# RWKV-7 recurrence and hard-swish layer: the decay scans of units 4 and 5 at another place in the order

## The chip, the cores and the metric

The kernel runs on one core of a Trainium2 chip. The metric is device microseconds of one execution. The engines are TensorE (PE; PEld is its weight load), VectorE (DVE), ScalarE (ACT), GpSimd (POOL) and SyncE (SP), which here only issues DMAs. Each engine works through its own instructions in the order of the program and waits where an operand or a buffer isn't ready.

## The reference

The input is r, k, v, w, a, b, each of 4 batches, 8 heads, 768 steps and 40 elements. For each batch and head a 40 x 40 state is carried through the steps:

```
for t in range(S):
    y[:, :, t] = einsum('bhd,bhde->bhe', rt, state)
    Sa = einsum('bhde,bhe->bhd', state, at)
    state = state * wt - outer(Sa, bt) + outer(vt, kt)
```

The result, reshaped to 3072 rows of 320, is x of a dense layer: h = x @ w_in (320 x 2048), g = h * clip(h + 3, 0, 6) / 6, out = g @ w_out (2048 x 320). The output is float32. The two weight matrices come in as 64-bit floats, which the kernel converts itself.

## The kernel before, in words

**Units.** The 768 steps are cut into blocks of 64. A unit is a pair of batches and one block: names[i] gives its block and pair. Four units make a group (NU = 4), two blocks by two pairs, and there are 24. Inside a unit the recurrence is written as matrix products. Scaling by the cumulated decay makes this possible; it is what the change moves.

**prepare(i)** (L534) makes what a unit needs apart from the state. Its stages that matter here:
- "W" (w_stage, L537): four TensorE transposes of the unit's w into a PSUM tile (L484), two copies into wm, one of them reversed (L545/L549 on VectorE or L547/L551 on ScalarE, by the unit's number), the load of a later unit's w (`fetch("W", following(i))`, L553: two DMAs on SyncE), and a scan into prods on VectorE (L555).
- "gam" (gam_stage, L560): a reciprocal (L564) and a scan backward (L566) on VectorE, then gam and rgam, the cumulated decay and its inverse: one half of each copied from wm by VectorE (L579, for units from 4 on), the other half from prods by GpSimd (L583, L584), and dec, by GpSimd too (L586).
- "A" (L593): transposes of a, which VectorE multiplies by gam into at (L599). "B" (L602) does the same for b and rgam (L607). "K", "F", "factor", "E" and "EV" follow.

**step(i)** (L832) carries the state through a unit: RT, VT (transposes), C, R, S, U, UT, rS (r against the old state), sn (the state sum, L961 and L969), H, y (L984; VectorE adds ys in L995 and GpSimd multiplies by gam in L996 into yg), and move, move2: eight DMAs on SyncE, four each (L1010, L1015), that bring yg into the layout of the dense layer (xt).

**Dense layer and weights.** feed_forward() (L1039) cuts the dense layer into pieces: h matmuls (L1066), ScalarE and VectorE for the hard-swish (L1081, L1082), o matmuls (L1107). pieces(n) issues n of them. load_weights() (L312) converts the weights in 20 parts: loads on SyncE (L334), three ScalarE activations each (power(), L384 to L386), three VectorE instructions each (L369, L372, L360). A piece may be issued only when its weights are converted in program order.

**Order.** The kernel fixes the order of every engine by hand. Around the change it is PLAN (L1282), a text of 16 lines. A word such as "2UT:1" runs stage UT of unit 2's step, with one part of the weight conversion dealt at its matmuls; X and Y are blocks of the first inversion; P and Q stand for prepare(4) and prepare(5) and run first "W", then "gam". From the ninth line on (t = 8) the PSUM for the dense layer is taken, and pieces and the second group's other stages (by_twos, L1197) go between the lines. By then ps_any (L119) hands out only two kinds of PSUM bank in turn: "one", which exists once, and a "pair", which exists twice.

```
1303  chains.update({x: in_turn(prepare(NU + n, None), ["W", "gam"]) for n, x in enumerate("PQ")})
1317          if t == BEGIN:
1318              fetch("A", NU + 1)
1319              fetch("W", NU + 3)
...
1331          if t >= BEGIN:
1332              next(second_group)
```

**Buffers the steps touch.** w of units 4 and 6 use one buffer (inputs["W"]); w of unit 5 is loaded early into values[4], the buffer that v of unit 4 gets later. ys and yg share two buffers (tag "yg"): unit 3's yg (L947, L990) gets the one that unit 2's yg leaves once its moves are done. wm exists twice, gam six times, rgam and prods twice.

Of the kernel before, what the change touches and what calls it, by code (L numbers as in the profile page):

```python
# [17 lines left out]
P = 128  # L18
# [13 lines left out]
def kernel(  # L32
# [47 lines left out]
    NU = 2 * NP  # L80
# [361 lines left out]
    def fetch(name, i, engine=None):  # L442

        if i is None or i >= NK:
            return
        x, crossed = {"W": (w, 0), "A": (a, 0), "B": (b, 0), "K": (k, 0), "R": (r, 1),
                      "V": (v, 1)}[name]
        if name == "V":
            t = values[i % AHEAD]
        else:  # L450
            t = placed.get((name, i))
            if (name, i) == ("R", 1):
                t = others["K"]
            if (name, i) == ("W", NU + 1):
                t = values[NU]
            t = t if t is not None else (others if i < 2 * NU and i % 2 and name != "R" else inputs)[name]
        g, p = names[i]
        engines = engine or nc.sync
        for q in range(2):
            engine = engines[q] if isinstance(engines, tuple) else engines  # L460
            y = x[2 * p + q, :, g * BL:(g + 1) * BL, :]
            rows = slice(q * BL, (q + 1) * BL)
            if crossed:
                for s in range(2):
                    engine.dma_start(out=t[rows, 4 * s:4 * s + 4, 0:D],
                                     in_=y[s::2].rearrange("h t e -> t h e"))
            else:
                engine.dma_start(out=t[rows, :, 0:D], in_=y.rearrange("h t e -> t h e"))  # L468
        data[i][name + "N"] = t

    def following(i):

        if i < 2:
            return None
        if i < 2 * NU:

            return i + 2 if i % NU < NU - 2 or i % 2 == 0 else None
        return i + 1

    def turn_pairs(x):  # L480

        o = ps_any([P, NPR, P])
        for n in range(NPR):
            nc.tensor.transpose(out=o[:, n, :],  # L484
                                in_=x[:, 2 * n:2 * n + 2, :].rearrange("p s e -> p (s e)"),
                                identity=ident[:])
        return o
# [46 lines left out]
    def prepare(i, F):  # L534
        n, o = i % NU, data[i]
        halves = i >= 2 * NU
        def w_stage():  # L537
            wt = turn_pairs(o["WN"])
            yield PE

            wm = o["wm"] = wms[i % 2]
            wv = wm[:, 0:SCAN].rearrange("p (r m i) -> p r m i", m=2, i=HB + 1)
            x = wt[:].rearrange("p r (q m i) -> p (r q) m i", q=2, m=2)
            if i in (0, NU, NU + 1):
                nc.vector.tensor_copy(wv[:, :, 0, 1:HB + 1], x[:, :, 0, ::-1])  # L545
            else:
                nc.scalar.activation(out=wv[:, :, 0, 1:HB + 1], in_=x[:, :, 0, ::-1], func=AF.Copy)  # L547
            if i in (0, NU, NU + 1):
                nc.vector.tensor_copy(wv[:, :, 1, 1:HB + 1], x[:, :, 1, :])  # L549
            else:  # L550
                nc.scalar.activation(out=wv[:, :, 1, 1:HB + 1], in_=x[:, :, 1, :], func=AF.Copy)  # L551
            if i != NU + 1:
                fetch("W", following(i))  # L553
            prods = o["prods"] = tmp.tile([P, NB, 2, HB + 1], F32, name="prods", bufs=2)
            nc.vector.tensor_tensor_scan(  # L555
                out=prods[:].rearrange("p r m i -> p (r m i)"), data0=wm[:, 0:SCAN], data1=start[:],
                initial=0.0, op0=ALU.mult, op1=ALU.add,
            )
# [135 lines left out]
        def ev_stage():  # L694
# [10 lines left out]
            for x in range(2):  # L705
                nc.scalar.activation(out=EV[half(x)], in_=ev[2][half(x)][:, ::-1] if x else ev[2][half(x)],  # L706
                                     func=AF.Copy)
            o["EV"] = EV

        return {"W": w_stage, "gam": gam_stage, "A": a_stage, "B": b_stage, "F": f_by_32 if i < 2 * NU else f_by_64,  # L710
                "factor": factor_stage, "K": k_stage, "E": e_stage, "EV": ev_stage}

# [559 lines left out]
    def block(i, j):  # L1272

        if i % NU < 2:
            if j == 0:
# [4 lines left out]


    PLAN = """X X:2 0U:4 0UT:2 1R  # L1282
              0sn:2 0H:1 Y:2 P
              1U 1UT:2 0y P
              2RT:1 Y:1 Q
              1sn:1 1H:1 2VT:2 0move 0move2
              1y:2 2R Q
              2S:3 3RT:2
              1move 1move2 2U:3 2UT:1 2C:5
              3R:4 3VT  # L1290
              2rS:3 2sn:3 2H:4 3S:2
              2y:3 3U:1 3UT:10 3C:5
              3rS:1 3sn:2 3H:4 2move
              3y:1 2move2

              3move
              3move2"""
# [191 lines left out]
```

## Time and profile before

| | |
|---|---|
| median of three runs | 792.41 us (791.11 to 794.02) |
| profiled execution | 788.99 us, its span 787.3 us |
| TensorE | 723.7 us busy, 92% of the span, 15832 matmuls |
| VectorE | 496.1 us, 63% |
| ScalarE | 320.0 us, 41% |
| GpSimd | 175.0 us, 22% |
| mean granted TensorE clock | 0.972 of full speed |
| chain that ended last, by engine | PE 77%, DVE 8%, issue 5%, SPq 4%, DMA 3%, ACT 2%, POOL 1% |

The page cuts the span in 40 equal slices and gives each engine's busy share in tenths, 9 for 90% or more. The timeline lists instructions in order of time: start and length in us, engine, line, operation, output and inputs by tile name, how many were merged, and in brackets the idle time of the engine before it and what ended that. A row of busy times by stretch gives for each stretch the busy us and count of each engine, the granted clock, the DMA share and GB/s. SPq is SyncE's issuing of DMAs. W loads appear as W<-in_w_dram for inputs["W"] and as WA<-in_w_dram for a second buffer that units 5 and 7 use.

### The profile page before, as it was taken

The numbers are of one execution on the slowest core, as the hardware profiler recorded it, in microseconds if no ns is written. First come the engines' busy times: TensorE is split into PE (matmuls) and PEld (weight loads), VectorE is DVE, ScalarE is ACT, GpSimd is POOL, SyncE is SP. The second block draws the span as 40 slices with busy tenths as digits, with TensorE's granted clock in tenths as the row PEclk, the third lists the DMA queues.
The fourth block names the chain that finished last, engine by engine and source line by source line (L and its number), as shares of the span: only waits on it lengthen the run. The fifth ranks groups of instructions, "written<-read, shape, count | busy, mean of one in ns | idle before, by whom it ended". The sixth has DMA issues, their size and how long they took to land.

```text
span 787.3 us, 35307 instructions
## 1 busy us (share of the span) xinstructions
PE 723.7 (92%) x15832; PEld 614.3 (78%) x15832; DVE 496.1 (63%) x971; ACT 320.0 (41%) x664; POOL 175.0 (22%) x318
## 2 busy tenths in 40 slices
PE   4626679999999989999999999999999999999998
PEld 3625668778778878888888888888888888888886
DVE  7899995598545699345888445987435982323210
ACT  2377982214445324444334534335534224412211
POOL 6403113122222304112404212304312201000000
PEclk9856999999999999999999999999999999999999
DMA  9684554411332313223213223213221101110000
GB/s 123 115 194 129 127 153 69 75 26 29 55 68 54 66 25 58 51 43 66 46 30 64 45 48 62 50 28 64 45 55 34 33 8 30 30 30 10 14 19 17
DMA packets 174215, 45.03 MB, mean 57 GB/s; under 512 B 157424, under 2 KB 172784, under 8 KB 174064
## 3 DMA queue, kind: packets, MB, share of 16 engines
q1 hardware_dynamic: 169760, 42.03, 27.8%
q8 instruction: 125, 2.05, 1.1%
q10 hardware_dynamic: 4304, 0.74, 0.7%
q14 instruction: 26, 0.21, 0.1%
HBM read 34.08 MB, written 3.93 MB: 48 GB/s over the span
## 4 chain that ended last, share of the span: by engine, by line
PE 77%; DVE 8%; issue 5%; SPq 4%; DMA 3%; ACT 2%; POOL 1%; DVEq 0%; POOLq 0%; ACTq 0%
PE h L1066 27%; PE o L1107 24%; PE pair L522 4%; PE pair L984 3%; PE pair L494 2%; PE pair L961 2%; PE one L484 2%; SPq L468 2%; PE pair L906 2%; PE pair L868 2%; DVE prod L753 1%; DVE x L759 1%; PE pair L926 1%; PE pair L942 1%; PE pair L701 1%
## 5 line engine op out<-in xcount | busy, mean ns | idle before, releaser
L1066 PE MATMUL h<-xt,win 128*128 128x128 f32 (+1 forms) x2304 | 249.2, 282 | 2.8 <-DVE gt L1082 2.0
L1066 PEld LDWEIGHTS h<-xt,win 128*128 128x128 f32 (+1 forms) x2304 | 229.9, 191 | 19.8 <-issue 5.0
L1107 PE MATMUL o<-wout,gt 128*128 128x320 f32 x768 | 230.4, 443 | 0.0
L1107 PEld LDWEIGHTS o<-wout,gt 128*128 128x128 f32 x768 | 138.4, 190 | 50.3 <-issue 0.2
L1082 DVE SCALAR_TENSOR_TENSOR gt<-gt,h 128x512 f32<-128x512 f32 x96 | 62.0, 681 | 71.4 <-ACT gt L1081 71.3
L1081 ACT ACTIVATE gt<-h,three 128x512 f32<-128x512 f32 x96 | 62.1, 685 | 101.9 <-PE h L1066 101.4
L996 POOL TENSOR_TENSOR yg<-ys,gam 128x512 f32<-128x512 f32 x22 | 39.0, 1774 | 156.3 <-DVE ys L995 83.6
L753 DVE TENSOR_TENSOR prod<-x 128x30 f32<-128x30 f32 (+9 forms) x180 | 67.2, 373 | 8.8 <-POOL x L738 3.3
L674 POOL TENSOR_TENSOR KBt<-K,rgt 128x320 f32<-128x320 f32 x22 | 19.0, 866 | 215.6 <-ACT rgt L663 177.8
L759 DVE TENSOR_TENSOR x<-x,prod 128x30 f32<-128x30 f32 (+9 forms) x180 | 62.2, 346 | 5.5
L969 DVE TENSOR_TENSOR state<-pair,state 40x320 f32<-40x320 f32 (+1 forms) x43 | 20.9, 487 | 60.8 <-PE pair L961 34.5
L530 DVE COPY_PREDICATED score<-mask,pair 128x512 f32<-128x512 int32 x72 | 50.6, 723 | 0.5
L995 DVE TENSOR_TENSOR ys<-pair,ys 128x512 f32<-128x512 f32 x22 | 15.2, 691 | 42.9 <-PE pair L701 21.8
L566 DVE TENSOR_TENSOR_SCAN wm<-wm,start 128x528 f32<-128x528 f32 x24 | 37.5, 1562 | 0.8
L555 DVE TENSOR_TENSOR_SCAN prods<-wm,start 128x528 f32<-128x528 f32 x24 | 30.1, 1259 | 10.4 <-ACT wm L551 10.3
L846 ACT ACTIVATE RT<-pair 128x512 f32<-128x512 f32 x22 | 13.1, 596 | 52.8 <-PE pair L494 52.8
L706 ACT ACTIVATE EV<-pair 64x320 f32<-64x320 f32 x44 | 19.0, 431 | 33.7 <-PE pair L701 23.0
L821 ACT ACTIVATE tinv<-pair 32x256 f32<-32x256 f32 x48 | 17.9, 374 | 31.7 <-PE pair L811 31.1
L1125 ACT ACTIVATE ob<-o 128x320 f32<-128x320 f32 x22 | 9.6, 435 | 49.4 <-PE o L1107 29.6
L583 POOL COPY gam<-prods 128x256 f32<-128x256 f32 x24 | 22.0, 916 | 30.7 <-DVE prods L555 26.9
L872 DVE TENSOR_TENSOR RR<-pair,EV 128x320 f32<-128x320 f32 x22 | 10.7, 487 | 25.4 <-PE pair L522 25.4
L984 PE MATMUL pair<-score,KBt 64*64 64x64 f32 x1408 | 25.9, 221 | 0.5 <-issue 0.5
(272 smaller groups left out, 1066.1 us busy)
## 6 DMA issues: line engine op xcount, KB each, us to landing
V<-in_v_dram SPq DMA_DIRECT2D x96, 40.0 KB
out_dram<-ob SPq DMA_DIRECT2D x47, 80.0 KB
R<-in_r_dram SPq DMA_DIRECT2D x92, 40.0 KB
B<-in_b_dram SPq DMA_DIRECT2D x42, 80.0 KB
K<-in_k_dram SPq DMA_DIRECT2D x42, 80.0 KB
W<-in_w_dram SPq DMA_DIRECT2D x37, 80.0 KB
A<-in_a_dram SPq DMA_DIRECT2D x37, 80.0 KB
xt<-yg SPq DMA_DIRECT2D x72, 40.0 KB
```

The costliest lines, as they stand in the source:

```text
L522: nc.tensor.matmul(out=o[i][half(q), n, :], lhsT=lhs[half(i, D), n ^ (2 * q * swap), half(q)], rhs=rhs[half(i, D), n, half(q)], start=True ...
L530: nc.vector.copy_predicated(out=x[:].rearrange("p (i h) t -> p i h t", i=2), mask=mask8, data=o[2])
L555: nc.vector.tensor_tensor_scan(out=prods[:].rearrange("p r m i -> p (r m i)"), data0=wm[:, 0:SCAN], data1=start[:], initial=0.0, op0=ALU.m ...
L566: nc.vector.tensor_tensor_scan(out=back, data0=back, data1=start[:], initial=0.0, op0=ALU.mult, op1=ALU.add)
L753: nc.vector.tensor_tensor(out=pv, in0=_ap(x[:], (i + 1) * L + i, [[L, n], [0, i]]), in1=_ap(x[:], i * L, [[0, n], [1, i]]), op=ALU.mult,)
L759: nc.vector.tensor_tensor(out=rest, in0=rest, in1=pv, op=ALU.add)
L984: nc.tensor.matmul(out=y[q][half(s), pr, :], lhsT=o[name][half(q), h * D:h * D + SLOT], rhs=m[name][half(q), 4 * rs + 2 * s + j, :], start ...
L996: nc.gpsimd.tensor_tensor(out=yg[:], in0=m["ys"][:].rearrange("p r q t -> p r (q t)"), in1=o["G"][:], op=ALU.mult)
L1066: nc.tensor.matmul(out=hp[c][:, i, :], lhsT=lhsT, rhs=rhs, start=(begun[c] == 0), stop=(begun[c] == 3 * NQ - 1))
L1081: nc.scalar.activation(out=gt[:], in_=hp[c][:], func=AF.Relu, bias=three[:], scale=1.0)
L1082: nc.vector.scalar_tensor_tensor(out=gt[:], in0=gt[:], scalar=6.0, in1=hp[c][:], op0=ALU.min, op1=ALU.mult)
L1107: nc.tensor.matmul(out=op[:], lhsT=gts[c][:, n, :], rhs=wout[:, c * HJ + r * NQ + n, :], start=((split or r == 0) and c == 0 and n == 0), ...
```

## The change

P and Q, the "W" and "gam" stages of units 4 and 5, leave the lines of PLAN in which units 0 and 1 step, and stand in the two lines that end unit 3: "W" of both behind 3H and ahead of 2move, "gam" of both behind 3y and ahead of 2move2. With them the two copies of "W" for these units go from VectorE to ScalarE, as for all other units but unit 0.

```diff
-            if i in (0, NU, NU + 1):
+            if i == 0:
                 nc.vector.tensor_copy(wv[:, :, 0, 1:HB + 1], x[:, :, 0, ::-1])
             else:
                 nc.scalar.activation(out=wv[:, :, 0, 1:HB + 1], in_=x[:, :, 0, ::-1], func=AF.Copy)
-            if i in (0, NU, NU + 1):
+            if i == 0:
                 nc.vector.tensor_copy(wv[:, :, 1, 1:HB + 1], x[:, :, 1, :])
...
     PLAN = """X X:2 0U:4 0UT:2 1R
-              0sn:2 0H:1 Y:2 P
-              1U 1UT:2 0y P
-              2RT:1 Y:1 Q
+              0sn:2 0H:1 Y:2
+              1U 1UT:2 0y
+              2RT:1 Y:1
               1sn:1 1H:1 2VT:2 0move 0move2
-              1y:2 2R Q
+              1y:2 2R
               2S:3 3RT:2
               1move 1move2 2U:3 2UT:1 2C:5
               3R:4 3VT
               2rS:3 2sn:3 2H:4 3S:2
               2y:3 3U:1 3UT:10 3C:5
-              3rS:1 3sn:2 3H:4 2move
-              3y:1 2move2
+              3rS:1 3sn:2 3H:4 P Q 2move
+              3y:1 P Q 2move2
```

The counts behind the colons are as before, and P and Q have none, so each part of the weight conversion and each piece of the dense layer stays where it was among the other stages.

## The prediction

> **What bounds the kernel now.** I read the slices of the page, then busy times by stretch, then SyncE's queue in order of time, then the other engines from 67 to 165 us, where all moved work lies. In the slices, each 19.7 us, TensorE is at 9 from the seventh on, and before that VectorE and ScalarE are:
>
> ```profile
> PE   4626679999999989999999999999999999999998
> ...
> DVE  7899995598545699345888445987435982323210
> ACT  2377982214445324444334534335534224412211
> ```
>
> So time lost once TensorE is full stays lost; time won before it moves the whole program forward. By stretch (columns: PE, PEld, DVE, ACT, POOL busy us with counts, granted clock, DMA share, GB/s):
>
> ```profile
> 74.40:115.40 41.00, 30.24 (x920) 26.96 (x922) 38.33 (x72) 37.59 (x62) 6.77 (x15) 0.96 0.58 148
> ...
> 119.00:127.00 8.00, 8.00 (x115) 6.22 (x105) 3.02 (x7) 1.09 (x3) 1.47 (x3) 1.00 0.32 56
> 127.00:142.00 15.00, 15.00 (x283) 12.60 (x282) 11.58 (x21) 4.09 (x9) 7.20 (x11) 1.00 0.40 71
> 142.00:148.00 6.00, 4.12 (x91) 3.79 (x89) 1.30 (x3) 1.89 (x5) 0.00 (x0) 1.00 0.46 80
> ```
>
> The work leaves the first stretch, where VectorE is busy for 38.3 of 41 us and ScalarE for 37.6. It arrives in the next two, where TensorE has no gap. The third holds a wait, read below. SyncE's queue (start, length, line, count of DMAs):
>
> ```profile
> 107.28 1.31 SPq L468 DMA_DIRECT2D WA<-in_w_dram  x2
> 112.62 3.10 SPq L1010 DMA_DIRECT2D xt<-yg  x4
> 116.80 2.02 SPq L468 DMA_DIRECT2D B<-in_b_dram  x2
> 118.93 1.28 SPq L468 DMA_DIRECT2D K<-in_k_dram  x2
> 120.25 3.41 SPq L1015 DMA_DIRECT2D xt<-yg  x4
> 123.71 5.30 SPq L465 DMA_DIRECT2D V<-in_v_dram  x8
> ```
>
> It idles from 108.6 to 112.6, and from 118.9 on it issues back to back, to 155.9. Three waits hang on it (idle time and releaser in brackets):
>
> ```profile
> 124.39 0.69 DVE L599 TENSOR_TENSOR at<-one,gam 128x512 f32<-128x512 f32 x1 [1.96 <-PE one L484]
> ...
> 125.06 1.27 POOL L996 TENSOR_TENSOR yg<-ys,gam 128x512 f32<-128x512 f32 x1 [5.92 <-DMA xt<-yg]
> ...
> 147.50 0.63 PE L484 MATMUL one<-ident,B 128*128 128x128 f32 x4 [1.88 <-DMA B<-in_b_dram]
> ```
>
> **What leaves the first stretch.** On VectorE, unit 4:
>
> ```profile
> 75.53 0.42 DVE L545 COPY wm<-one 128x256 f32<-128x256 f32 x1
> 75.86 0.41 DVE L549 COPY wm<-one 128x256 f32<-128x256 f32 x1
> 76.31 1.26 DVE L555 TENSOR_TENSOR_SCAN prods<-wm,start 128x528 f32<-128x528 f32 x1
> ```
>
> From the first copy to the next other instruction (77.49) is 1.96 us; the gamma part (reciprocal, scan, memset, two copies) runs from 78.89 to 80.88, 1.99. Unit 5 takes 1.95 (82.22 to 84.17) and 1.99 (88.66 to 90.65). Together VectorE is relieved of 7.9 us. TensorE loses eight transposes (0.44 us for four), GpSimd six copies (1.24 and 1.30 us), SyncE the two DMAs of unit 6's W at 80.75 (1.33 to the next issue).
>
> ScalarE keeps all it has there, and it idles only 41.0 - 37.6 = 3.4 us. So the gain lies between 0 and 3.4 us if ScalarE bounds, against 7.9 if VectorE does. Two of ScalarE's gaps should go: 1.11 us at 106.38 (L1081 waits for h, behind unit 3's state transposes, behind the state sum that VectorE reaches only at 102.86) and 0.36 at 79.89. Then the state matmul at 117.57, which waited 0.86 us for a mask on VectorE, gains some 0.5. I take **2.0 us**, the nearer row being ScalarE's. That RT of unit 2 now takes another PSUM bank and shifts the later ones is an edit I cost at nothing, within the same bounds, since evacuations on ScalarE pace these banks.
>
> **What arrives.** Times here are still those of before; the 2.0 comes off at the end. Four copies go to ScalarE (0.39 us each by L547), which idles 8.1 us until 125.90: nothing. Transposes of W4 and W5 go behind unit 3's H (ends 119.2); 0.87 us, inside the wait below.
>
> The load of W6 is the part that counts. It writes the buffer that W4 is read from, so it must wait for W4's transposes, now at about 119.65. On SyncE it stands ahead of unit 2's first four moves, which went at 112.62. Behind it come, by pitches of the same queue at 135 to 145 us: W 1.38, four moves 3.14, B 1.45, K 1.37, second moves 2.58, together 9.92. So the second moves end at 129.6 instead of 123.66, and land 1.40 later (as 123.66 to 125.06), at 131.0.
>
> L996 of unit 3 waits for that landing, since its buffer is unit 2's. Now GpSimd's gamma copies stand behind it: 131.0 + 1.27 for L996 + 0.40 for L583 gives 132.6, at of unit 4 takes 0.69 to 133.3. VectorE's own part (two scans, two gammas, 1.26 + 1.26 + 2 x 1.99, with L995 0.69, from 120.0 on) is done by 127.5 and is hidden by that wait; were the wait gone, it alone would hold at until 128.2. The transposes of W6 write the one bank that at reads, so TensorE stands until 133.4 instead of starting them at 125.70: **7.7 us**.
>
> At 147.50 TensorE waited 1.88 us for B6. That wait is absorbed if the load isn't later: from 129.6 it is V 5.34, R 2.70, A 1.4 to 2.3, A 1.37, W 1.38, moves 3.14 and 2.58, so 147.5 to 148.4, and 4.99 to use (142.51 to 147.50) gives 152.5 to 153.4. TensorE comes at 145.62 + 7.7 = 153.3. So **7.7 - 1.9 = 5.8** is left. The next gap, 1.54 us at 161.36, waits on VectorE's inversion, which starts as much later; after it TensorE is full.
>
> **The clock.** The idle stretch, 126.6 to 133.4, is long enough to lower the granted clock, as these rows show for a stretch half idle:
>
> ```profile
> 159.00:162.00 3.00, 1.46 (x66) 1.16 (x65) 2.86 (x5) 0.00 (x0) 3.00 (x5) 1.00 0.01 4
> 162.00:165.00 3.00, 3.00 (x40) 1.81 (x36) 2.86 (x9) 0.86 (x2) 0.28 (x1) 0.57 0.63 109
> 165.00:168.00 3.00, 3.00 (x27) 2.98 (x24) 2.76 (x8) 0.86 (x2) 0.00 (x0) 0.86 0.26 60
> ```
>
> There four o matmuls took 2.11 us against 1.34, the EV matmuls 1.09 against 0.68, 48 h matmuls 5.29 against 4.83: 1.6 us in all. Between 0 and 2.5 (clock low for longer) I take **1.6**. The Trainium skill (TensorE: Matmul & The Clock Gate, Part 1: The HAM clock gate) says that the clock halves after an idle window of about 3.4 us and is full again only after a busy one. By it an idle stretch of 6.8 us must hold such a window, and the loss, an estimate from that page, is about 1.7 us. The trace agrees: 0.57 and 0.86 over 3 us each make 3.4 us at half clock.
>
> **Sum.** 5.8 + 1.6 - 2.0 = +5.4 us. The profiled execution took 788.99 (span 787.3 and 1.7 around it), which gives 794.4; the median of the runs, 792.41, is 3.4 higher, and on it I forecast **797.8**. With 3.4 won and no clock loss it is +2.4, with nothing won and 2.5 of clock and 1 of load +9.3.
>
> **Rivals.**
> 1. *The load queue alone.* L996 doesn't hold the gammas (if its buffer came free another way). Then TensorE gets W6 at about 128.3, but B6 still lands at 152.5 to 153.4, 5.0 to 5.9 late, with or without a clock drop: 5.0 - 2.0 = +3.0, 795.4. For it: SyncE is continuous in either case. Against: the bracket of 125.06.
> 2. *SyncE isn't held* (ends faster). If W6's load doesn't wait for W4, it fits into SyncE's idle 108.6 to 112.6 (1.38 of 4.0), and yg, loads and clock stay. The price is VectorE's own chain: W6 at 128.3, +2.6, less the 1.9 of B6, less 2.0: -1.3, 791.1. It decides from the point where that load issues before 112.6. Against it: one buffer serves both.
> 3. *VectorE bounds the first stretch.* 7.9 won in place of 2.0: 5.8 + 1.6 - 7.9 = -0.5, 791.9. For it: 38.3 of 41 busy. Against: ScalarE's 37.6, unchanged.
> 4. *More is lost*: loads land late beside others, or the clock falls twice: +10, 802.4.
>
> **Chances.** Forecast 0.62, rivals 1 to 4: 0.16, 0.08, 0.07, 0.07. Half a per cent (4.0 us) is about what a measurement of this kernel can tell from no change. Of the forecast's own bounds (+2.4 to +9.3) some four fifths lie above it; with rival 4 and a little of rival 1 slower has 0.64. Rivals 2 and 3 lie within half a per cent save with the early gain at its greatest: faster 0.06, the same 0.30. The range, 793.5 to 802.0, leaves rivals 2, 3 and most of 4 out.
>
> **What would show it.** Right: W6's DMAs on SyncE just behind W4's transposes, with an idle stretch of some 7 us ahead of them; L996 of unit 3 still waiting for xt<-yg and GpSimd's gamma copies behind it; TensorE idle 6 to 7 us before W6's transposes and the clock low for 3 us after; B6's wait gone; unit 3's H some 2 us earlier. Wrong: W6's load ahead of the moves without a wait; H earlier by 5 us or more; at of unit 4 released by VectorE's copies instead of GpSimd's; or TensorE's idle time filled, which no queued work there allows, since it issues in order.

## The result and the profile after

The changed kernel took 798.19 us (median of five runs, 796.59 to 800.38) against 792.1 (790.97 to 794.02) for the kernel before in the same session: 1.0082 of it, with a 95% interval of 1.0058 to 1.0105. That is 6.1 us more by the medians. The profiled execution took 799.9 us, its span 798.2.

The slices of the page after, each 20.0 us:

```profile
PE   5726776999999989999999999999999999999998
...
DVE  7898876689546699445798355888444983322210
ACT  2386881322553424452334454334444324412111
```

VectorE has lost work in the fourth to sixth slices, ScalarE a little in the fourth and fifth. TensorE, at 9 from the seventh slice on before, stands at 6 there now (120 to 140 us) and is full only from the eighth. What holds it in the seventh begins in SyncE's queue:

```profile
107.94 2.10 SPq L468 DMA_DIRECT2D WA<-in_w_dram  x2
121.95 1.27 SPq L468 DMA_DIRECT2D W<-in_w_dram  x2
123.32 3.55 SPq L1010 DMA_DIRECT2D xt<-yg  x4
126.97 1.37 SPq L468 DMA_DIRECT2D B<-in_b_dram  x2
...
129.76 2.54 SPq L1015 DMA_DIRECT2D xt<-yg  x4
```

SyncE issues nothing from 110.0 to 122.0. Then the load of W6 goes, and unit 2's moves, which before went at 112.6, follow it. The last of them is issued by 132.30, and the engines that hang on it come late (start, length, engine, line, and the idle time with its releaser in brackets):

```profile
133.78 1.26 POOL L996 TENSOR_TENSOR yg<-ys,gam 128x512 f32<-128x512 f32 x1 [12.50 <-DMA xt<-yg]
134.99 0.40 POOL L583 COPY gam<-prods 128x256 f32<-128x256 f32 x1
...
135.42 0.69 DVE L599 TENSOR_TENSOR at<-one,gam 128x512 f32<-128x512 f32 x1 [5.77 <-POOL gam L583]
...
136.17 1.12 PE L484 MATMUL one<-ident,W 128*128 128x128 f32 x4 [7.34 <-DVE wm L596]
...
137.93 1.84 PE L1066 MATMUL h<-xt,win 128*128 128x128 f32 x8
...
158.07 0.60 PE L484 MATMUL one<-ident,B 128*128 128x128 f32 x4
```

GpSimd's L996 waits for the moves, its gamma copy L583 stands behind it, VectorE's at waits for that copy, and TensorE idles for 7.34 us ahead of W6's transposes, until at has read their bank (the bracket names L596, the small fill issued behind at; at ends at 136.11). The transposes and the h matmuls behind them are slow (1.12 and 1.84 us; four transposes take 0.60 at 158.07). At that last line, B6, TensorE waits for nothing, where before it waited 1.88 us. The clock by stretch (columns as before: PE, PEld, DVE, ACT, POOL, granted clock, DMA share, GB/s):

```profile
74.40:115.40 41.00, 31.71 (x928) 28.41 (x920) 29.39 (x52) 35.32 (x58) 3.58 (x8) 0.79 0.55 145
...
132.00:135.00 3.00, 0.00 (x0) 0.00 (x0) 0.00 (x0) 0.00 (x0) 1.22 (x2) 0.62 0.21 38
135.00:138.00 3.00, 1.83 (x9) 1.83 (x10) 1.42 (x3) 0.63 (x2) 1.78 (x8) 0.50 0.36 59
138.00:141.00 3.00, 3.00 (x22) 3.00 (x22) 1.84 (x2) 0.69 (x3) 0.00 (x0) 0.74 0.40 64
```

In the first row, the stretch that the work left, VectorE is down from 38.3 to 29.4 us of 41, and ScalarE only from 37.6 to 35.3. Not all of that is the change: a second profile of the kernel before has 34.4 and 33.0 there, at a granted clock of 0.75 where the first has 0.96. The others show the idle stretch and the fall of the clock.

**A measure for the rest.** Absolute times of two profiles differ ahead of the late part: the kernel before starts unit 3's H (the L522 pair behind the state sum) at 118.52 us in the first profile and at 123.26 in a second one, copies_act below at 126.63. So I count from that start, called H, to W6's transposes, to those of unit 7's B (B7, close behind B6's), and to the end of the span. The waits of TensorE for B6 and for B7, both on a load, stand together. What comes behind B7 takes 637.8 to 641.1 us in these profiles, a spread whose cause is known only in part (three of them, before, copies_act and gam_late, hold a fall of the clock that the last section describes). So H to B7 is the safer measure of the late part, and H to the end the rougher one:

| kernel | ratio to before (95%) | H | H to W6 | idle at W6 | waits at B6 + B7 | H to B7 | H to end |
|---|---|---|---|---|---|---|---|
| before | 1 | 118.52 | 7.18 | 0 | 1.88 + 0 | 30.56 | 668.8 |
| before, second profile | | 123.26 | 7.18 | 0 | 0 + 1.50 | 30.06 | 667.8 |
| after | 1.0082 (1.0058 to 1.0105) | 120.66 | 15.51 | 7.34 | 0 | 38.74 | 677.5 |
| w6_behind | 1.0038 (1.0020 to 1.0055) | 121.49 | 10.91 | 2.74 | 0 | 33.75 | 673.7 |
| gam_ahead | 1.0062 (1.0038 to 1.0086) | 120.73 | 10.21 | 2.03 | 4.54 + 0 | 38.44 | 677.8 |
| both | 1.0016 (0.9997 to 1.0035) | 121.09 | 10.21 | 2.04 | 0 | 33.06 | 671.2 |
| copies_act | 1.0006 (0.9983 to 1.0029) | 126.63 | 7.18 | 0 | 1.51 + 1.13 | 31.25 | 671.1 |
| left_out | 0.9994 (0.9975 to 1.0013) | 120.27 | 7.89 | 0 | 0.18 + 1.29 | 30.81 | 669.8 |
| queue_only | 1.0069 (1.0046 to 1.0092) | 120.84 | 8.01 | 0 | 5.05 + 0 | 37.12 | 678.3 |
| gam_late | 1.0023 (1.0004 to 1.0042) | 122.59 | 7.20 | 0 | 1.52 + 1.13 | 31.29 | 670.2 |
| moves_behind_after | 1.0061 (1.0037 to 1.0084) | 120.30 | 15.76 | 7.60 | 0 | 38.39 | 677.2 |
| moves_behind_gam | 0.9982 (0.9959 to 1.0006) | 120.81 | 10.21 | 2.03 | 0 | 32.02 | 670.5 |
| moves_behind_before | 0.9961 (0.9937 to 0.9985) | 119.59 | 7.18 | 0 | 0 | 28.41 | 666.2 |
| turns_kept | 1.0054 (1.0029 to 1.0078) | 120.37 | 15.07 | 6.90 | 0 | 38.92 | 676.8 |

### The profile page after: what moved, and what is told of

It reads as the page before. It is cut to its first block, busy times and chain, and to the rows that moved or that the text cites. A ratio compares the mean times of both kernels' runs of the same rounds, so it can differ in the third digit from the quotient of the medians.

```text
span 798.2 us, 35317 instructions
## 1 busy us (share of the span) xinstructions
PE 730.6 (92%) x15832; PEld 620.6 (78%) x15832; DVE 494.7 (62%) x967; ACT 321.3 (40%) x668; POOL 174.3 (22%) x318
## 4 chain that ended last, share of the span: by engine, by line
PE 76%; DVE 12%; issue 4%; ACT 3%; DMA 2%; SPq 2%; POOL 1%; DVEq 0%; POOLq 0%; ACTq 0%
PE h L1066 25%; PE o L1107 22%; PE pair L522 4%; PE pair L984 3%; PE one L484 3%; DVE prod L753 3%; DVE x L759 2%; PE pair L961 2%; PE pair L494 2%; PE pair L906 2%; PE pair L868 1%; PE pair L926 1%; PE pair L942 1%; PE pair L811 1%; DVE wm L566 1%
## 5 line engine op out<-in xcount | busy, mean ns | idle before, releaser
L1081 ACT ACTIVATE gt<-h,three 128x512 f32<-128x512 f32 x96 | 62.1, 685 | 97.9 <-PE h L1066 97.4
L996 POOL TENSOR_TENSOR yg<-ys,gam 128x512 f32<-128x512 f32 x22 | 39.0, 1771 | 165.4 <-DVE ys L995 80.9
L566 DVE TENSOR_TENSOR_SCAN wm<-wm,start 128x528 f32<-128x528 f32 x24 | 37.7, 1570 | 0.8
L821 ACT ACTIVATE tinv<-pair 32x256 f32<-32x256 f32 x48 | 18.0, 374 | 31.7 <-PE pair L811 31.1
L984 PE MATMUL pair<-score,KBt 64*64 64x64 f32 x1472 | 28.4, 225 | 0.8 <-issue 0.8
L984 PEld LDWEIGHTS pair<-score,KBt 64*64 64x64 f32 x1472 | 24.8, 138 | 3.5 <-issue 1.8
```

Source lines behind the costliest of these rows:

```text
L566: nc.vector.tensor_tensor_scan(out=back, data0=back, data1=start[:], initial=0.0, op0=ALU.mult, op1=ALU.add)
L984: nc.tensor.matmul(out=y[q][half(s), pr, :], lhsT=o[name][half(q), h * D:h * D + SLOT], rhs=m[name][half(q), 4 * rs + 2 * s + j, :], start ...
L996: nc.gpsimd.tensor_tensor(out=yg[:], in0=m["ys"][:].rearrange("p r q t -> p r (q t)"), in1=o["G"][:], op=ALU.mult)
L1081: nc.scalar.activation(out=gt[:], in_=hp[c][:], func=AF.Relu, bias=three[:], scale=1.0)
```

## The experiments

The theory on trial is the forecast's: SyncE, held by W6's load, makes unit 2's moves late, and they hold the gammas through L996 (called the yg link below), while the early gain is small. The rivals are that the queue of loads alone costs it, that VectorE's own late work does, and that the early gain is large. One per cent is 7.9 us.

**w6_behind.** The load of W6 goes behind the first moves and the loads of B and K, so that SyncE isn't held. The gammas stay behind L996.

```diff
-            if i != NU + 1:
+            if i not in (NU, NU + 1):
                 fetch("W", following(i))
...
                 fetch(name, NU + 1)
+            fetch("W", NU + 2)
```

> The changed kernel, with one edit: unit 6's W is loaded behind unit 5's K instead of in W of unit 4, so SyncE doesn't wait for W4's transposes ahead of unit 2's moves. Theory A (as predicted: the held load queue makes yg, and behind it the gamma copies, late): unit 2's moves go some 9 us earlier against unit 3's H, L996 of unit 3 waits about 5 to 6 us as before and not 12.5, TensorE's idle time ahead of W6's transposes falls from 7.3 to about 2 or 3 us, the clock stays full there, and the time falls by about 7 us to 790 to 792. Theory B (VectorE's late scans and gammas alone hold TensorE, SyncE only goes along): idle time ahead of W6 stays at 5 us or more, and the time stays above 796.

Measured: 1.0038, about half of the loss gone. Its timeline, GpSimd first and then TensorE:

```profile
129.91 1.26 POOL L996 TENSOR_TENSOR yg<-ys,gam 128x512 f32<-128x512 f32 x1 [7.80 <-DVE wm L566]
```
```profile
132.40 0.66 PE L484 MATMUL one<-ident,W 128*128 128x128 f32 x4 [2.74 <-DVE wm L596]
...
133.33 1.72 PE L1066 MATMUL h<-xt,win 128*128 128x128 f32 x8
```

L996 starts 8.4 us behind H, against 13.1 after and 6.5 before. The bracket names VectorE's scan L566, but that scan ends at 129.92, when L996 has begun. SyncE's queue shows the likelier releaser:

```profile
124.75 3.69 SPq L1015 DMA_DIRECT2D xt<-yg  x4
```

The last of these moves is issued by 128.44, 1.47 us ahead of L996, and in after the same distance is 1.48. So L996 still follows the moves, with W6's load now just ahead of the second ones. VectorE's late chain ends about level with GpSimd's: the last gamma copy of VectorE at 131.74, the first of GpSimd at 131.59, and at starts at 131.69. W6 comes 10.91 us behind H, against 7.18 before. The clock falls here too: 1.72 us for eight h matmuls that take 1.06 at full clock. So the held queue costs a good part, though the 790 to 792 expected were missed, and VectorE's late chain and what is left of the yg link share the rest.

**gam_ahead.** GpSimd's gamma copies go ahead of L996; the queue stays held.

```diff
-              3y:1 P Q 2move2
+              P Q 3y:1 2move2
```

> The changed kernel, with one edit: in the last line of unit 3, both gammas stand ahead of y instead of behind it, so GpSimd's gamma copies don't stand behind L996. The load of W6 still holds SyncE. Theory A (two links: yg ahead of the gamma copies, and the load queue itself): at of unit 4 comes some 6 us earlier, released by VectorE's own copies, but B6 still lands as late as in the changed kernel, so TensorE waits 3 to 5 us for it at B6's transposes; 795 to 797. Theory A' (the yg link is the whole loss): no new wait at B6, 791 to 793. Theory C (the load queue is the whole loss): 798, unchanged.

Measured: 1.0062, which can't be told from after's 1.0082. The idle time at W6 shrinks to 2.03 us, and comes back at B6:

```profile
130.94 0.66 PE L484 MATMUL one<-ident,W 128*128 128x128 f32 x4 [2.03 <-DVE wm L596]
...
156.45 1.08 PE L484 MATMUL one<-ident,B 128*128 128x128 f32 x4 [4.54 <-DMA B<-in_b_dram]
157.33 1.92 PE L1066 MATMUL h<-xt,win 128*128 128x128 f32 x8
```

Cutting the yg link alone gives next to nothing, since the late load takes its place 25 us later, and its 4.54 us are long enough for the clock to fall as well (1.92 us for eight h matmuls).

**both.** The two edits above together.

> The changed kernel with both edits: W6's load behind unit 5's K, and the gammas ahead of y. Theory A: at of unit 4 is paced by VectorE's chain, as with the load moved alone; 789.5 to 792, within 1 us of it. If GpSimd's order still cost something once SyncE is free, this one is 1 to 2 us under the load moved alone.

Measured: 1.0016 (0.9997 to 1.0035), 1.3 us above before. TensorE idles 2.04 us at W6, behind VectorE alone, and B6 and B7 wait for nothing. The time stays above the 789.5 to 792 that were expected, but the two edits together take away most of the loss (1.0082), and neither gets as far alone.

**copies_act.** The kernel before with only the first half of the change: ScalarE makes the four copies of units 4 and 5, at their early place.

```diff
-            if i in (0, NU, NU + 1):
+            if i == 0:
```

> The kernel before, with one edit: the four copies of W of units 4 and 5 are made by ScalarE instead of VectorE, at their old place among the steps of units 0 and 1. It moves 1.6 us of work from VectorE to ScalarE. Theory D (ScalarE paces that stretch): unit 3's H comes 1 to 2 us later, time +1 to +2 us, about 793.7. Theory E (VectorE paces it): H 1 to 2 us earlier, time about 790.5.

Measured: 1.0006 (0.9983 to 1.0029). The 1.7 us that were to be won if VectorE paced the first stretch (0.9979) lie just outside, the 1 to 2 us that were to be lost if ScalarE did lie inside, and so does nothing at all. It speaks against VectorE and settles no more. H at 126.63 in its profile, which took 799.46 us and was the slowest of twelve executions (790.55 at the least), shows how far one execution of the early part can be from another.

**before_again.** The kernel before, once more, for a second profile.

> The kernel before, unchanged, for a second profile. Where unit 3's H starts varies with the granted clock between 72 and 84 us: the first profile (788.99 us, H at 118.5) had it full from 75 us on, the four profiles of kernels with late scans not before 81 to 90 us. If that is chance, H comes between 119 and 123 here; if the early transposes of W4 and W5 keep the clock up, H is at 118 to 119 again.

Measured: 792.83 us, span 791.1. H is 4.7 us later than in the first profile, and H to W6 is the same to 0.01 us. The wait at B6 stands at B7 here, 1.50 us.

**left_out.** The early gain by itself: the moved work isn't done at all, units 4 and 5 use the gammas of units 0 and 1, and W6 is loaded where it was. The edit is one of after.

```diff
-              3rS:1 3sn:2 3H:4 P Q 2move
-              3y:1 P Q 2move2
+              3rS:1 3sn:2 3H:4 2move
+              3y:1 2move2
...
-    chains.update({x: in_turn(prepare(NU + n, None), ["W", "gam"]) for n, x in enumerate("PQ")})
+    for n in range(2):
+        data[NU + n].update(G=data[n]["G"], rg=data[n]["rg"], dec=data[n]["dec"], wm=wms[n])
...
+        if t == 1:
+            fetch("W", NU + 2)
```

> The kernel before without the moved work: the scans and gammas of units 4 and 5 are left out wholly, early and late (these units use the gammas of units 0 and 1, so the values are not the reference's), and W6 is loaded at its old place. Its gain over the kernel before is what the relief of the first stretch is worth, with nothing paid later. Theory D (ScalarE paces the stretch, the prediction's 2.0): 1 to 3.4 us, ratio 0.996 to 0.999. Theory E (VectorE paces it): 7 to 8 us, ratio 0.990 to 0.991. Theory F (no relief, since the clock or the weight loads set the pace): 0.

Measured: 0.9994 (0.9975 to 1.0013), that is 0.5 us won (2.0 won to 1.0 lost). VectorE's 7.9 us are gone from the stretch and the time hardly moves:

```profile
74.40:115.40 41.00, 33.00 (x943) 29.77 (x935) 29.99 (x53) 35.85 (x59) 3.71 (x8) 0.75 0.61 154
```

VectorE's time turned into idle time, 11.0 of 41 us. That VectorE bounds the first stretch, which would have won 7.9 us, is ruled out. The gain isn't quite alone here: H to B7 is 0.3 to 0.8 us longer than in the two profiles of before.

**queue_only.** left_out with the held queue put back: only the transposes of W4 and W5 stand behind unit 3's H, and W6's load behind them. No scan, no gamma, no yg link.

```diff
+    def turned_only(i):
+        turn_pairs(data[i]["WN"])
+        if i == NU:
+            fetch("W", NU + 2)
+        yield DONE
...
+    chains.update({x: turned_only(NU + n) for n, x in enumerate("PQ")})
```

> The kernel with the moved work left out, plus only the transposes of W4 and W5 behind unit 3's H and W6's load behind them; no late scan, no late gamma (values not the reference's). It adds the hold of SyncE and nothing else. If the load queue alone is the loss: TensorE reaches W6's transposes at most 1 us late but waits 4 to 6 us for B6, and the time is 5 to 7 us over the kernel with the work left out, that is 3 to 5 us over before, ratio 1.004 to 1.006. If the yg link was needed: within 1 us of the kernel with the work left out.

Measured: 1.0069 (1.0046 to 1.0092), above the 1.004 to 1.006 expected. The held queue alone costs as much as the whole change, as far as the intervals tell. Its two places on TensorE:

```profile
128.85 0.60 PE L484 MATMUL one<-ident,W 128*128 128x128 f32 x4
...
155.30 1.09 PE L484 MATMUL one<-ident,B 128*128 128x128 f32 x4 [5.05 <-DMA B<-in_b_dram]
```

W6 without a wait, then 5.05 us for B6, and the clock down there (1.09 us for four transposes). By H to B7, too, it costs nearly what after does: 37.12 against 38.74, and 30.06 to 30.56 before.

**gam_late.** The kernel before with the gammas of units 4 and 5 late, ahead of 3y. The transposes, the scans and W6's load stay early, so no link of the forecast is there.

```diff
-              1U 1UT:2 0y P
+              1U 1UT:2 0y
...
-              1y:2 2R Q
+              1y:2 2R
...
-              3y:1 2move2
+              P Q 3y:1 2move2
```

> The kernel before, with the W stages of units 4 and 5 left where they are, and only their gammas late, ahead of unit 3's y. VectorE is relieved early of 4.0 us, W6's load stays at its old place on SyncE, and VectorE's late chain is two gammas, 4.0 us. Theory A with D: at of unit 4 comes at most 1 us later against H, SyncE isn't held, the early gain is about 1 us: ratio 0.998 to 1.001. If late gammas alone cost what the change cost: 1.005 or more.

Measured: 1.0023 (1.0004 to 1.0042), 1.8 us more than before, where at most 1.001 was expected. W6 comes 7.20 us behind H, as in before. B6 and B7 wait 2.65 us together, 0.8 to 1.2 more than in the two profiles of before. That is about half of the 1.8. Behind B7 its profile has a fall of the clock at a wait of 1.55 us (166.16), which one of the two profiles of before has as well; nothing shows that the edit brings it, and the interval nearly takes in nothing.

**moves_behind_after.** This takes the late loads away and leaves the yg link. Ahead of the loads for units 6 and 7 (B among them), SyncE issues unit 3's eight moves and R of unit 4: 12 DMAs that nobody needs so soon. They go behind those loads.

```diff
-              3move
-              3move2"""
+"""
...
-            fetch("R", NU)
...
+    for name in ("move", "move2"):
+        for _ in stages[3][name]():
+            pass
+    fetch("R", NU)
     for _ in weights:
```

> The changed kernel, with one edit: on SyncE, unit 3's eight moves and unit 4's R (12 DMAs, which nobody needs before 165 us) stand behind the loads of B and K of units 6 and 7 instead of ahead of them. The hold by W6's load and the yg link stay as they are; B6 is loaded some 8 us earlier. If the two links overlap, each enough for the whole loss: TensorE still idles about 7 us ahead of W6's transposes, there is no wait at B6, and the time stays at 796.5 to 799, ratio 1.006 to 1.009. If late loads were the whole loss and the yg link only shifted the idle time, the time falls to 791 to 793.5.

Measured: 1.0061 (1.0037 to 1.0084), no different from after as far as the intervals tell.

```profile
136.06 1.12 PE L484 MATMUL one<-ident,W 128*128 128x128 f32 x4 [7.60 <-DVE wm L596]
```

There is no wait at B6 and B7, and the loss sits at W6 alone: the yg link, too, is enough by itself.

**moves_behind_gam.** The same edit on gam_ahead: SyncE is still held, but neither what hangs on the moves nor what hangs on the loads is needed soon.

> The changed kernel with the gammas ahead of unit 3's y and the same 12 DMAs behind the loads of units 6 and 7: the yg link is off the gammas and B6 isn't late, while W6's load still holds SyncE. If the two links are the loss: idle 2 to 3 us ahead of W6's transposes (VectorE's chain), no wait at B6, ratio 1.000 to 1.003, as with both edits on W6 and the gammas. If something else is lost: 1.005 or more.

Measured: 0.9982 (0.9959 to 1.0006), under the 1.000 to 1.003 expected; the next run shows that this edit wins time on the kernel before as well.

```profile
131.02 0.66 PE L484 MATMUL one<-ident,W 128*128 128x128 f32 x4 [2.03 <-DVE wm L596]
```

What hung on SyncE is gone, here and at B6 and B7; the 2.03 us that VectorE costs are left. With its neighbours this makes a square, ratios to before:

| | loads of units 6, 7 late | loads early |
|---|---|---|
| gammas behind L996 | after 1.0082 | moves_behind_after 1.0061 |
| gammas ahead of L996 | gam_ahead 1.0062 | moves_behind_gam 0.9982 |

One link costs about what both do: a TensorE that is late at W6 isn't made to wait at B6.

**moves_behind_before.** The same edit on the kernel before.

> The kernel before, with the same 12 DMAs behind the loads of units 6 and 7. In before TensorE waits 1.9 us for B6, and the queue ahead of it is these DMAs. The wait goes: 0.997 to 0.999, about 791. If the next wait takes its place (VectorE's inversion behind F): 1.000.

Measured: 0.9961 (0.9937 to 0.9985), median 789.7 us: 3.1 us faster than before (1.2 to 5.0), and the fastest of all. Here SyncE's queue shows the new order:

```profile
135.84 1.28 SPq L468 DMA_DIRECT2D B<-in_b_dram  x2
...
141.62 3.10 SPq L1010 DMA_DIRECT2D xt<-yg  x4
```

and neither B6 nor B7 waits. In the two profiles of before those waits took 1.88 and 1.50 us, which lies inside the interval of the gain; if there is more to it, it isn't traced. Against this base the change with the same edit costs 1.0061/0.9961 = 1.0100, or 8 us, and with the gammas ahead of L996 0.9982/0.9961 = 1.0021, or 1.7 us (each give or take 0.0034, the two intervals combined as independent).

**turns_kept.** after, with the eight transposes of W4 and W5 made at their old places as well, unused. It asks whether TensorE's work there sets the clock, and with it the early part.

```diff
+    def turned_early(i):
+        turn_pairs(data[i]["WN"])
+        yield DONE
...
-              0sn:2 0H:1 Y:2
+              0sn:2 0H:1 Y:2 M
...
-              2RT:1 Y:1
+              2RT:1 Y:1 N
```

> The changed kernel, with the eight transposes of W4 and W5 also left at their old places among the steps of units 0 and 1 (done twice, the early result unused). It restores TensorE's work and the order of the PSUM banks in the first stretch, and nothing else. If these set the clock or the banks there, the clock is full from about 75 us on and the time falls by 1 to 4 us, ratio to before 1.003 to 1.007. If the clock's rise there is chance: 1.007 to 1.009, as the changed kernel.

Measured: 1.0054 (1.0029 to 1.0078), which overlaps with after's interval. The clock does rise earlier, though not by the transposes (below), and H at 120.37 comes no earlier than after's 120.66. Whether the transposes are worth anything stays open.

## Why the prediction was right

It said 797.8, and the medians gave 798.19. The late mechanism was the forecast's, step for step. That the number is within 0.4 us is luck: the interval of the ratio alone is 1.9 us to either side, and the size of the early gain isn't settled.

- **The early gain, 2.0 us: not settled, and its steps held in part.** The forecast let two of ScalarE's gaps and the wait at the mask go. In after and left_out L1081's gap (1.11 us; 2.11 in before's second profile) is gone, but the small one at L821 (0.36) stands at 0.32 and 0.44, and the wait at the mask (0.86) at 0.79 and 0.85. left_out measures 0.5 in all (2.0 won to 1.0 lost), and 0.8 to 1.3 if its longer late part is added back. H some 2 us earlier, one of the forecast's signs, can't be read: 120.66 lies between the two profiles of before. The granted clock of 0.75 in left_out is no sign of a price either, since before's second profile has 0.75 as well. The forecast took ScalarE's 37.6 of 41 us from one profile, and the other has 33.0.
- **W6's load and the queue: right.** Counted from H, the load went at 1.29 us (forecast 1.13), the second moves were issued by 11.64 (11.05), L996 started at 13.12 (12.45). The 14 DMAs took 10.35 us from the first issue to the last, forecast 9.92.
- **TensorE's delay at W6, 7.7 us: right.** H to W6 grew by 8.3, the extra 0.6 from the queue.
- **The clock, 1.6 us: right.** From W6's transposes to W7's took 3.44 us against 1.77, so 1.67. The granted clock of 0.62, 0.50 and 0.74 over three stretches of 3 us makes (0.38 + 0.50 + 0.26) x 3 / 0.5 = 6.8 us at half clock, of which the last 3.4 fall behind 136.17, where TensorE works. The Trainium skill's windows of about 3.4 us (TensorE: Matmul & The Clock Gate, Part 1: The HAM clock gate) agree: this is two of them.
- **B6's wait, 1.9 us: right.** After doesn't wait there, nor at B7. In the second profile of before the wait is 1.50 us at B7 instead, so the credit is 1.5 to 1.9 us. To see all of the late part at once, take H to B7: 30.56 and 30.06 us in the two profiles of before, 38.74 after. It grew by 8.2 and 8.7; the forecast had 5.8 + 1.6 = 7.4.
- **The sum.** By the runs the late part costs 1.0082/0.9994 = 1.0088, 7.0 us, give or take 2.4; H to B7 says 8.2 and 8.7. The forecast's 7.4 agrees with the first and is about 1 short of the second. The net is 6.5 us by the ratio (6.1 by the medians), against 5.4. Taken with H to B7 it leaves 1.7 to 2.2 us won elsewhere, which fits the forecast's 2.0; taken with left_out it leaves 0.5. The runs don't decide between the two.

**The rivals.** *The load queue alone* was priced at +3.0 us; queue_only gives 1.0069, +5.5. Its term of 5.0 us was right (5.05 measured), but that wait, too, drops the clock, which the price left out; and of the 2.0 of early gain it is not known how much was there. So it isn't the mechanism of after, where B6 doesn't wait, and would cost the same if the other were cut: a rival that stands in line behind the forecast. *SyncE isn't held* was priced at -1.3 us; both, which has that and no yg link, gives +1.3, w6_behind +3.0. The price left out that VectorE's late chain (H to W6 longer by 3.0 and 3.7 us, forecast 2.6) brings a fall of the clock, which both and w6_behind show, and again it took 2.0 of early gain. *VectorE bounds the first stretch* is ruled out by left_out. *More is lost* didn't come.

## What to carry to other kernels

When work is moved back, follow the loads that wait for its buffers: on a queue that issues in order, one load that waits holds up all the DMAs behind it (SyncE issued nothing from 110.0 to 122.0 in after), and here that alone cost as much as the whole change (queue_only 1.0069). Two waits that hang on one cause may cover each other, so that cutting either brings little; cut them one at a time and together before judging a mechanism by its share. And look at what stands on such a queue ahead of the load that a wait names: putting 12 DMAs that nobody needed yet behind it made the kernel before 0.9961 of its time.

## What the runs showed of the hardware

**A gap of 2.04 us can drop the clock, and so can one of 1.54.** In both, TensorE idled from 129.26 to 131.30; in gam_ahead from 128.91 to 130.94. The stretch behind, of both and then of gam_ahead:

```profile
132.00:135.00 3.00, 3.00 (x19) 3.00 (x18) 1.84 (x2) 0.98 (x4) 0.12 (x2) 0.61 0.36 60
```
```profile
132.00:135.00 3.00, 3.00 (x30) 3.00 (x29) 2.62 (x3) 1.01 (x4) 1.26 (x2) 1.00 0.22 38
```

The clock fell in the one, some 1.4 us after work had resumed, and not in the other (nor in moves_behind_gam, 2.03 us). At 0.61 and then 0.82 over 3 us each it was at half for (0.39 + 0.18) x 3 / 0.5 = 3.4 us, which costs 1.7. w6_behind fell after 2.74 us of idle time (0.76 and 0.68). The Trainium skill (TensorE: Matmul & The Clock Gate, Why this matters for your kernels) advises against gaps of more than about 3 us; these runs show the fall at shorter ones. The shortest stand in the kernel before. Its wait for VectorE's inversion, 1.54 us at 161.36, drops the clock in the first profile: the prediction's rows on the clock show this fall, so what agrees there is its length of 3.4 us, and not an idle window of that length ahead of it. In the second profile the same wait, 0.02 us longer, leaves the clock full, and four o matmuls take 1.34 us where they took 2.11:

```profile
165.59 0.68 PE L701 MATMUL pair<-V,score 64*64 64x40 f32 x32 [1.56 <-DVE score L530]
166.19 1.34 PE L1107 MATMUL o<-wout,gt 128*128 128x320 f32 x4
```

All 14 profiles have this wait, at 1.39 to 1.56 us, and the clock falls behind it in three (before, copies_act, gam_late). The same page (Part 1) says that the window runs freely, so that the outcome would depend on where in it the gap lies; equal gaps with unequal outcomes are what that would look like, and these cases don't prove it.

**The early rise of the clock isn't the transposes' work.** In four profiles the clock is full from 75 to 78 us: before, both times, moves_behind_before and turns_kept. In turns_kept:

```profile
75.00:78.00 3.00, 1.16 (x60) 0.92 (x55) 1.17 (x2) 2.90 (x6) 0.00 (x0) 1.00 0.63 178
```

The other ten are at 0.50 there, among them all eight without the early transposes of W4 and W5, which makes the transposes look like the cause. But the clock rises first: in the four it is full by 73.0 to 74.0 us, and W4's transposes start at 73.86 to 74.46, at 73.86 in turns_kept, where the clock was full from 73.0. In gam_late and copies_act, which have them too, the clock is still at 0.50 when they start (75.62 and 77.73). What sets the rise isn't shown. No difference in H goes with it, so here it cost nothing that could be measured.
